# Forms of x summed in PSUM, and the part up to the second pair ordered by the scheduler

## The chip, the core and the metric

The kernel runs on one core of one Trainium2 chip. The metric is device time in microseconds, from the runs of a whole execution. PE is the matrix engine (TensorE), DVE the vector engine, ACT the scalar engine, POOL GpSimd, and SP the engine that issues most transfers. PSUM is the memory into which PE writes; SBUF is the working memory.

## What is computed

An attention without a score matrix feeds a layer of eight experts, and that feeds a feed-forward layer. Batch 4, 8 heads, sequence 576, head width 64; 2304 tokens of width 512.

```python
q_s = exp(q - max(q, -1)); q_s /= sum(q_s, -1) + 1e-9
k_s = exp(k - max(k, 2));  k_s /= sum(k_s, 2) + 1e-9      # over the sequence
x   = q_s @ (k_s^T v)                                     # per batch and head
# x: [2304, 512]
P = exp(x @ w_gate - max); 8 times: rows to 1, columns to 1, times N/E
out = sum over e of P[:, e] * (relu(x @ w1[e]) @ w2[e])   # 8 experts, 512 -> 1024 -> 512
h = out @ w_in; g = h * clip(h + 3, 0, 6) / 6             # 512 -> 2048
return g @ w_out                                          # -> 512
```

## The kernel before

Tokens lie in six groups of 384 (GN); a pair of groups is the unit of the expert products: PAIRS is (0, 1), (3, 4), (2, 5). Batches 0 and 1 give groups 0 to 2 (attention object `t0`), batches 2 and 3 give groups 3 to 5 (`t1`). The hidden width is cut into 20 slices of 512 (16 of experts, 4 of the last layer). A step (s, p) multiplies pair p by slice s: `up_burst` (L845) in two halves of seven sums in PSUM banks A, B, C, D, A, B, C, and `down_tile` (L918) into bank tag d for six token tiles. Values are kept as a high and a low half in f16, and each product is three f16 products.

The up product of a pair uses seven products of combined blocks instead of eight. For each pair x is cut into four blocks, b11 and b21 (channel halves of the first group) and b12 and b22 (of the second), and seven forms of them are stored, with high and low half, in `xop[p]`: QB11, QB21, QB22 are blocks, T1 = b12 - b11, T2 = b22 - T1, T4 = T2 - b21, T3 = b22 - b12. cp = 0, 1 counts two channel quarters of a half, so there are 14 forms in a pair. `combine_steps` (L365) makes them: `xmm` (L593 to L605) multiplies k^T v (`bds`) by the turned q (`qT`, L592) on PE, and ACT writes the sum to SBUF times a power of two `sx`; DVE subtracts (L379); ACT writes the high half (L374) and DVE or POOL the low half (L375).

`sx` comes from the largest element of k^T v over all partitions (`kvmax`, `across_max`, `pow2` at L190 to L199). The third pair has one group of each attention object: group 2's x is kept unscaled in `stage2` and scaled later (L676), with the larger maximum of both.

The order. The code is cut into blocks. Inside `with tc.manual_schedule()` every engine's instructions keep the order of the code; outside, a scheduler orders them at build time, with the order of the code as priority, and waits are set for either. Steps of other work are put in the queue `ticks`, and `tick()` after each product of the burst takes `rate` of them, which interleaves the code. Before the change two hand-ordered blocks stand at the beginning: one up to the first pair's x, and one (from L1110) with w1 and w2 of slice 1, group 2's x, steps (0, 0) and (1, 0), the second attention (`beside`, `pair_steps(1)`) and the down tiles of step (1, 0). Then the steps (0, 1), (0, 2), (1, 1), (1, 2) with the third pair, the gate's logits and the balancing (`sinkhorn_steps`) are scheduled. SP issues the second k (L418), then w1 of slice 1 (L260), the second v (L439), the second q (L418), w2 of slice 1 (L296). The buffers of k and v (`kt`, `vt`) lie in the room of the second and third pair's forms, those of q in `acc`.

Of the kernel before, what the change touches and what calls it, by code (L numbers as in the profile page):

```python
# [40 lines left out]
def tile_attention_moe_ffn(  # L41
# [12 lines left out]
    nc = tc.nc  # L54
    B, H, S, D = q.shape
    NT, DM = out.shape
# [42 lines left out]
    def psm(shape, name, dt=F32):  # L99
        return ps_m.tile(shape, dt, tag="m", name=name)  # L100
# [3 lines left out]

    ident = cpool.tile([P, P], F32, name="ident")
    ones = cpool.tile([P, P], F32, name="ones")
    three = cpool.tile([P, 1], F32, name="three")
    X_W = 7 * 2 * 2 * GN // 2
    W1_W = 7 * 2 * 2 * (FS // 2) // 2
# [10 lines left out]
    bds = cpool.tile([P, 2, NKC, P], F32, name="bds")  # L120
    sx = cpool.tile([P, len(PAIRS), 2], F32, name="sx")
    mx = cpool.tile([P, len(PAIRS)], F32, name="mx")
    prob = cpool.tile([P, NJ, E], F32, name="prob")
    lg = cpool.tile([P, NJ, 2 * E], F32, name="lg")
    win32 = dram.tile([DM, NF * FS], F32, name="win32")
# [42 lines left out]
    def run(steps):  # L168
        for f in steps:
            if f is not None:  # L170
                f()
# [190 lines left out]
        put(back, [], "conv")  # L362


    def combine_steps(p, cp, bs, first=False):  # L365
# [12 lines left out]
        def tt(o, a, b):  # L378
            return lambda: V.tensor_sub(o, a, b)  # L379

        if first:
            return [
                sp(QB11, b11, V), tt(t1, b12, b11),
                lambda: (tt(t2, b22, t1)(), sp(QT2, t2, V)()),
                sp(QT1, t1, V),
                lambda: (tt(t1, t2, b21)(), sp(QT4, t1, V)()),
                sp(QB21, b21, V),
                lambda: (tt(b12, b22, b12)(), sp(QT3, b12, V)()),
                sp(QB22, b22, V),
            ]  # L390
# [17 lines left out]
    def attention(pr):  # L408
# [126 lines left out]
        def kvkeep():  # L535
            nc.vector.tensor_copy(mx[:, pr : pr + 1], st["mm"])
            pow2(st["mm"], sx[:, pr, :], TOP1)
            if pr == 1:
                nc.vector.tensor_max(mx[:, 2:3], mx[:, 0:1], mx[:, 1:2])
                pow2(mx[:, 2:3], sx[:, 2, :], TOP1)  # L540


        gl = lambda g: g % (QR // GJ)
# [36 lines left out]
        def qtr(c, g, src=None):  # L580
            src = t["qn"] if src is None else src
            ps = psm([P, GJ, P], f"qT{c}_{g}")
            for r in range(GJ):
                nc.tensor.transpose(ps[:, r, :], src[:, r * P : (r + 1) * P], ident)
            t["m"] = t.get("m", 0) + 1
            if "rooms" in t:
                qT = t["rooms"][2 + t["m"] % 2]
# [6 lines left out]
        def xmm(c, g, dst, scale):  # L594
            if "rooms" not in t:
                t["x"] = t.get("x", -1) + 1
                ps = ps_u.tile([P, 512], F32, tag="CDAB"[t["x"] % 4], name=f"x{c}_{g}")[:, :GN]
                ps = ps.rearrange("p (r n) -> p r n", n=P)
            else:
                ps = psm([P, GJ, P], f"x{c}_{g}")  # L600
            q3 = t["qT", c, g].rearrange("p (r n) -> p r n", n=P)
            for i in range(2):
                n = slice(i * QP, (i + 1) * QP)
                nc.tensor.matmul(ps[:, :, n], bds[:, i, c, :], q3[:, :, n], start=True, stop=True)  # L604
            nc.scalar.activation(dst, ps.rearrange("p r n -> p (r n)"), AF.Copy, scale=scale)  # L605

        def items(lst):

# [3 lines left out]
            for u in range(n + late):  # L612
                def f(u=u):
# [10 lines left out]
        t["max"] = [lambda: (kvmax(), a()), gap, b, kvkeep]  # L624
        t.update(vcopy=vcopy, v_ones=v_ones, load_k=load_k, load_v=load_v, load_q=load_q, kmax=kmax, ktr=ktr, mT=mT,
                 kback=kback, ksub=ksub, kexp=kexp, kv_=kv, kvout=kvout, qmax=qmax, qsub=qsub, qexp=qexp, qsum=qsum,
                 qn_=qn, qtr=qtr, xmm=xmm, items=items)
        return t

    def call(t):  # L630
# [27 lines left out]
    def unit_items(p, cp, bs):  # L658
        ga, gb = PAIRS[p]
        x = sx[:, p, 0:1]  # L660
        return [(cp, ga, bs[0], x), (cp + 2, ga, bs[1], x), (cp, gb, bs[2], x), (cp + 2, gb, bs[3], x)]

    def pair_steps(p, items):
        steps = []
        for cp in range(2):
            if p < 2:
                bs = (U, R)[cp][:6]
                steps += items(unit_items(p, cp, bs))
            else:
                bs = [stage2[:, cp], stage2[:, cp + 2]] + U[2:6]  # L670
                gb = PAIRS[p][1]

                x = sx[:, 2, 0:1]

                def scaled(b):
                    return lambda: nc.scalar.activation(b, b, AF.Copy, scale=x)  # L676
                if cp == 0:
                    steps += group_steps(t1, gb)
                steps += [scaled(bs[0]), scaled(bs[1])]
                steps += items([(cp, gb, bs[2], x), (cp + 2, gb, bs[3], x)])  # L680
            steps += combine_steps(p, cp, bs)
        return steps

# [290 lines left out]
    with tc.manual_schedule():  # L974
        make_identity(nc, ident)
        nc.vector.memset(ones, 1.0)
        nc.vector.memset(three, 3.0 * KAPPA)
        nc.gpsimd.memset(bds, 0.0)

        t0, t1 = attention(0), attention(1)  # L980
        K = call(t0)
        w2_room = half(acc[:, :NFC, :])
        room1 = half(acc[:, NFC : 2 * GJ + GJ, :])
        U1 = [room1[:, i * GN : (i + 1) * GN] for i in range(6)]
# [34 lines left out]
        def turned(g):  # L1019
            for c in range(NKC + 1):  # L1020
# [15 lines left out]
        run(t0["max"][1:])  # L1036
        t1["load_k"](2)

        bs0, bs1 = U[:6], U1
        it = {(c, g): (c, g, dst, x) for c, g, dst, x in unit_items(0, 0, bs0) + unit_items(0, 1, bs1)}  # L1040
        c0 = combine_steps(0, 0, bs0, first=True)
        c1 = combine_steps(0, 1, bs1, first=True)
        X = lambda c, g: (lambda: t0["xmm"](*it[c, g]))
# [63 lines left out]


    FROM, TO, AGAIN = 6, len(order) - 3 * NF - 3, len(order) - 3 * NF + 2
    with tc.manual_schedule():  # L1110
        w1_1 = w1_steps(1)
        w1_1[0]()
        for i in range(2):
            t1["load_v"](i=i)
        t0["rooms"] = [U[3], U[4], U1[0], U1[1]]
        third = PAIRS[2][0]
        it = t0["items"]([(c, third, stage2[:, c], 1.0) for c in range(NKC)])
        put(ticks, a2, ("w2", 0))
        put(ticks, group_steps(t0, third))
        both = w1_1[4:]  # L1120
        while it or both:
            if both:
                put(ticks, [both.pop(0)])
            if it:
                put(ticks, [it.pop(0)])
        put(ticks, [], ("w1", 1))
        rate[0] = 3
        prev = step(0, 0, None)
        need(("w1", 1))
        t1["load_q"]()  # L1130
        w2_1 = w2_steps(1)
        w2_1[0]()
        t1["rooms"] = R[6:]
        one = beside(t1)
        put(ticks, one[:10])
        put(ticks, w2_1[4:], ("w2", 1))
        put(ticks, one[10:])
        put(ticks, pair_steps(1, t1["items"]), ("x", 1))
        rate[0] = 2
        prev = step(1, 0, prev)  # L1140
        for grp in range(2):
            run(downs(prev, grp))
        need(("x", 1))
        rate[0] = 1
        first_pair, prev = prev, None
# [3 lines left out]
    put(ticks, pair_steps(2, t1["items"]), ("x", 2))  # L1149
    put(ticks, logit_steps(1))  # L1150
    put(ticks, logit_steps(2))
    put(ticks, sinkhorn_steps(), "P")
# [45 lines left out]
```

## Time and profile before

| what | us |
|---|---|
| three runs | 1936.97, 1944.75, 1945.9 |
| median | 1944.75 |
| profiled execution, whole | 1942.0 |
| its span, first to last instruction | 1940.2 |
| PE busy in the span | 1847.7 (95%) |
| DVE busy | 1316.9 (68%) |
| ACT busy | 779.7 (40%) |
| POOL busy | 623.7 (32%) |

The profile is of one execution. Its page has the busy share of each engine in 40 slices of 48.5 us, and tables of groups of instructions. The trace is asked for more: stages (busy time of each engine between two moments), the timeline, waits, and groups by line. Times in it count from the span's start.

### The profile page before, as it was taken

The numbers are of one execution on the slowest core, as the hardware profiler recorded it, in microseconds if no ns is written. First come the engines' busy times: TensorE is split into PE (matmuls) and PEld (weight loads), VectorE is DVE, ScalarE is ACT, GpSimd is POOL, SyncE is SP. The second block draws the span as 40 slices with busy tenths as digits, with TensorE's granted clock in tenths as the row PEclk, the third lists the DMA queues.
The fourth block names the chain that finished last, engine by engine and source line by source line (L and its number), as shares of the span: only waits on it lengthen the run. The fifth ranks groups of instructions, "written<-read, shape, count | busy, mean of one in ns | idle before, by whom it ended". The sixth has DMA issues, their size and how long they took to land.

```text
span 1940.2 us, 26715 instructions
## 1 busy us (share of the span) xinstructions
PE 1847.7 (95%) x10506; PEld 987.0 (51%) x10506; DVE 1316.9 (68%) x2331; ACT 779.7 (40%) x1448; POOL 623.7 (32%) x588
## 2 busy tenths in 40 slices
PE   4569999999999999999999999999999999999999
PEld 3335545555555555555555555555555555555554
DVE  7685665776767667676667676666756897668554
ACT  3534543333434333333434343333333456544342
POOL 3214323433323323333323334242332323323111
PEclk9779999999999999999999999999999999999999
DMA  8710000121020111111111111111100100000001
GB/s 240 119 45 1 1 22 23 43 67 55 23 71 31 63 32 45 55 60 55 39 55 39 55 39 55 39 46 47 60 28 1 44 22 22 23 22 23 1 27 72
DMA packets 48622, 87.71 MB, mean 45 GB/s; under 512 B 12400, under 2 KB 12400, under 8 KB 48496
## 3 DMA queue, kind: packets, MB, share of 16 engines
q1 hardware_dynamic: 46800, 82.47, 14.0%
q10 hardware_dynamic: 1696, 3.54, 0.6%
q8 instruction: 82, 1.34, 0.3%
q14 instruction: 44, 0.36, 0.1%
HBM read 72.89 MB, written 13.11 MB: 44 GB/s over the span
## 4 chain that ended last, share of the span: by engine, by line
PE 79%; DVE 12%; DMA 3%; ACT 2%; issue 2%; POOL 1%; ACTq 0%; SPq 0%; DVEq 0%; POOLq 0%
PE y L918 41%; PE B L845 11%; PE C L845 10%; PE A L845 10%; PE D L845 5%; DVE r L853 2%; DVE w1buf L205 2%; DVE g L868 1%; DMA raw<-in_moe_w_dram 1%; DVE xbuf L375 1%; DVE scr L379 1%; DVE w2buf L205 1%; DVE acc L928 1%; PE x L604 1%; DMA acc<-in_moe_w_dram 1%
## 5 line engine op out<-in xcount | busy, mean ns | idle before, releaser
L918 PE MATMUL y<-w2buf,h 128*128 128x512 f16 x4320 | 980.1, 380 | 0.1
L845 PEld LDWEIGHTS <-w1buf 128*128 128x128 f16 x5040 | 494.9, 98 | 389.7 <-issue 47.6
L918 PEld LDWEIGHTS <-h 128*128 128x128 f16 x4320 | 423.2, 98 | 476.3 <-issue 4.8
L875 POOL TENSOR_TENSOR h<-r,h 128x384 f16<-128x384 f32 x288 | 276.1, 959 | 870.9 <-ACT h L874 799.8
L853 DVE SCALAR_TENSOR_TENSOR r<-B,r 128x384 f32<-128x384 f32 x240 | 133.2, 555 | 252.2 <-PE B L845 243.9
L928 DVE SCALAR_TENSOR_TENSOR acc<-y,cf,acc 128x512 f32<-128x512 f32 x252 | 188.3, 748 | 156.6 <-PE y L918 156.4
L845 PE MATMUL C<-xbuf,w1buf 128*128 128x384 f16 x1440 | 277.5, 329 | 15.2 <-DVE r L853 13.8
L845 PE MATMUL B<-xbuf,w1buf 128*128 128x384 f16 x1440 | 278.8, 330 | 8.0 <-DVE r L853 2.3
L845 PE MATMUL A<-xbuf,w1buf 128*128 128x384 f16 x1440 | 277.2, 328 | 5.4 <-ACT scr L605 4.3
L891 ACT ACTIVATE r<-A 128x384 f32<-128x384 f32 x120 | 58.8, 490 | 337.3 <-PE A L845 337.3
L873 ACT ACTIVATE r<-r 128x384 f32<-128x384 f32 x192 | 100.0, 521 | 165.5 <-DVE r L853 159.1
L874 ACT CAST h<-r 128x384 f16<-128x384 f32 x288 | 147.1, 511 | 8.6
L870 POOL TENSOR_TENSOR h<-g,h 128x384 f16<-128x384 f32 x72 | 67.7, 940 | 255.1 <-ACT h L869 204.5
L845 PE MATMUL D<-xbuf,w1buf 128*128 128x384 f16 x720 | 137.9, 326 | 3.4 <-DVE xbuf L375 1.1
L853 DVE SCALAR_TENSOR_TENSOR r<-C,r 128x384 f32<-128x384 f32 x240 | 132.6, 552 | 11.6 <-PE C L845 1.7
L884 ACT ACTIVATE r<-A 128x384 f32<-128x384 f32 x120 | 58.6, 488 | 203.4 <-PE A L845 203.4
L869 ACT CAST h<-g 128x384 f16<-128x384 f32 x96 | 49.1, 511 | 96.8 <-DVE g L868 96.8
L877 ACT ACTIVATE h<-r 128x384 f16<-128x384 f32 x96 | 50.1, 522 | 92.4 <-DVE r L853 92.4
L878 DVE SCALAR_TENSOR_TENSOR h<-r,h 128x384 f16<-128x384 f32 x96 | 81.5, 849 | 5.5 <-ACT h L877 5.5
L868 DVE SCALAR_TENSOR_TENSOR g<-g,r 128x384 f32<-128x384 f32 x96 | 62.4, 652 | 12.9 <-ACT g L867 10.4
L867 ACT ACTIVATE g<-r,three,zi 128x384 f32<-128x384 f32 x96 | 67.5, 704 | 7.6 <-DVE r L853 3.2
L853 DVE SCALAR_TENSOR_TENSOR r<-D,r 128x384 f32<-128x384 f32 x120 | 66.8, 556 | 3.9
(610 smaller groups left out, 1483.5 us busy)
## 6 DMA issues: line engine op xcount, KB each, us to landing
raw<-in_moe_w_dram SPq DMA_DIRECT2D x31, 1024.0 KB, 5.6
scr<-in_moe_w_in_dram SPq DMA_DIRECT2D x16, 512.0 KB, 4.2
scr<-in_moe_w_out_dram SPq DMA_DIRECT2D x16, 512.0 KB, 3.8
out_dram<-acc SPq DMA_DIRECT2D x18, 256.0 KB, 2.0
win<-scr SPq DMA_DIRECT2D x16, 256.0 KB, 3.4
wout<-scr SPq DMA_DIRECT2D x16, 256.0 KB, 2.2
raw<-win SPq DMA_DIRECT2D x4, 1024.0 KB, 5.0
raw<-wout SPq DMA_DIRECT2D x4, 1024.0 KB, 5.7
```

The source lines that it names most:

```text
L845: nc.tensor.matmul(bank[b], w[:, i, wi, c, fs], x[:, i, xi, c, :], start=(first and n == 0), stop=(last and n == 5), skip_group_check=True,)
L853: nc.vector.scalar_tensor_tensor(out=o, in0=bank[b], scalar=sign * H_DOWN, in1=i1, op0=ALU.mult, op1=ALU.add)
L867: nc.scalar.activation(r, c, AF.Relu, scale=zi, bias=three)
L868: nc.vector.scalar_tensor_tensor(out=r, in0=r, scalar=6.0 * KAPPA, in1=c, op0=ALU.min, op1=ALU.mult)
L870: eng.tensor_sub(h[:, 1, :], r, h[:, 0, :])
L873: nc.scalar.activation(c, c, AF.Relu)
L874: nc.scalar.copy(h[:, 0, :], c)
L875: eng.tensor_sub(h[:, 1, :], c, h[:, 0, :])
L878: nc.vector.scalar_tensor_tensor(out=h[:, 1, :], in0=c, scalar=0.0, in1=h[:, 0, :], op0=ALU.max, op1=ALU.subtract)
L891: nc.scalar.activation(r4, bank["A"], AF.Copy if ffn else AF.Relu, scale=H_DOWN)
L918: nc.tensor.matmul(ps, hs[grp][fc][:, hi, ts_], w[:, wi, fc, :], start=(n == 0), stop=(n == 11))
L928: nc.vector.scalar_tensor_tensor(out=acc[:, j, :], in0=ps, scalar=cf, in1=acc[:, j, :], op0=ALU.mult, op1=ALU.add)
```

## The change

The forms are no longer made in SBUF. k^T v is scaled once, when its scale is known. PE writes a block into a PSUM bank, and adds stored halves of other forms to it with an identity matrix (`plus`) or its negative (`minus`) in f16; ACT writes the high half from PSUM and DVE the low half. The bank of b22 is kept for T2, T4 and T3, which are further sums onto it. In the first pair the two kept banks are A and B and the others C, D and d; in the second they are the two buffers of tag m. The first pair's forms come in another order, as do w1's splits between them. The second pair's eight turned q get eight rooms instead of two, and their turning is written ahead of most forms. The second block is no longer hand-ordered; its text is the same but for that. The third pair's forms are made as before, with factors relative to the scales already in.

```diff
+        nc.scalar.copy(plus, ident)
+        nc.scalar.activation(minus, ident, AF.Copy, scale=-1.0)
         t0, t1 = attention(0), attention(1)
...
         def kvkeep():
             nc.vector.tensor_copy(mx[:, pr : pr + 1], st["mm"])
             pow2(st["mm"], sx[:, pr, :], TOP1)
+            nc.scalar.activation(bds[:, 0], bds[:, 0], AF.Copy, scale=sx[:, pr, 0:1])
+            nc.vector.tensor_scalar_mul(bds[:, 1], bds[:, 1], sx[:, pr, 0:1])
...
+        def xset(ps, c, g):
+            p3 = ps.rearrange("p (r n) -> p r n", n=P)
             q3 = t["qT", c, g].rearrange("p (r n) -> p r n", n=P)
             for i in range(2):
                 n = slice(i * QP, (i + 1) * QP)
+                nc.tensor.matmul(
+                    p3[:, :, n], bds[:, i, c, :], q3[:, :, n], start=(i == 0), stop=(i == 1), skip_group_check=True
+                )
...
+        def forms(p, cp, bank):
...
+            def out_(ps_, qd):
+                nc.scalar.copy(dst[:, qd, 0, cp], ps_)
+                nc.vector.tensor_tensor(out=dst[:, qd, 1, cp], in0=ps_, in1=dst[:, qd, 0, cp], op=ALU.subtract)
+
+            def onto(ps_, qds):
+                for m, qd in qds:
+                    for hl in range(2):
+                        nc.tensor.matmul(
+                            ps_, m, dst[:, qd, hl, cp], start=False, stop=True, skip_group_check=True
+                        )
...
+            return [
+                plain(cp, ga, QB11), f_t1, plain(cp + 2, gb, QB22), f_on(QT2, [(minus, QT1)]),
+                plain(cp + 2, ga, QB21), f_on(QT4, [(minus, QB21)]), f_on(QT3, [(plus, QB21), (minus, QB11)]),
+            ]
...
+    def second_pair(t):
...
+        f = [t["forms"](1, cp, lambda n: psm([P, GN], n)) for cp in range(2)]
...
-        run([X(0, ga), X(1, ga), c0[0], c1[0], a1[0], X(0, gb), X(1, gb), c0[1], c1[1], X(2, gb), X(3, gb), a1[1],
-             c0[2], c1[2], X(2, ga), X(3, ga), a1[2], c0[3], c1[3], a1[3], c0[4], c1[4], a1[4], c0[5], c1[5], a1[5],
-             c0[6], c1[6], a1[6], c0[7], c1[7]])
+        f0 = t0["forms"](0, 0, lasting("A"))
+        f1 = t0["forms"](0, 1, lasting("B"))
+        run([f0[0], f1[0], a1[0], f0[1], f1[1], f0[2], f1[2], a1[1], f0[3], f1[3], a1[2], f0[4], f1[4], a1[3],
+             f0[5], f1[5], a1[4], f0[6], f1[6], a1[5], a1[6]])
...
-    with tc.manual_schedule():
-        w1_1 = w1_steps(1)
-        w1_1[0]()
...
-        t1["rooms"] = R[6:]
...
-        put(ticks, pair_steps(1, t1["items"]), ("x", 1))
...
+    w1_1 = w1_steps(1)
+    w1_1[0]()
...
+    t1["rooms"] = R[8:] + R[:8]
...
+    put(ticks, second_pair(t1), ("x", 1))
```

## Rows read from the trace of the kernel before

**Rows 1.** The page's slices of 48.5 us: busy tenths, granted clock in tenths

```profile
PE   4569999999999999999999999999999999999999
PEclk9779999999999999999999999999999999999999
```

**Rows 2.** Stages: from:to, length, busy (instructions) of PE, PEld, DVE, ACT, POOL; clock; transfers

```profile
42.50:51.50 9.00, 4.34 (x26) 3.82 (x25) 5.51 (x12) 6.49 (x14) 0.00 (x0) 0.95 0.03 9
51.50:135.00 83.50, 48.01 (x206) 25.17 (x206) 65.15 (x109) 39.50 (x70) 18.91 (x18) 0.72 0.47 84
135.00:190.00 55.00, 50.22 (x516) 29.82 (x515) 31.41 (x58) 25.99 (x50) 20.31 (x21) 0.94 0.05 17
190.00:270.00 80.00, 73.99 (x575) 43.95 (x573) 59.67 (x158) 40.43 (x80) 26.04 (x27) 1.00 0.02 4
...
51.50:66.00 14.50, 10.56 (x38) 4.65 (x37) 12.88 (x28) 11.16 (x22) 1.45 (x1) 0.74 0.00 0
```

**Rows 3.** Waits of PE, 51.5 to 135 us: total us, times, longest

```profile
PE kT L463 <- DVE scr L456: 19.2, 4, 9.4
PE C L845 <- DVE r L853: 9.2, 2, 6.1
```

**Rows 4.** Timeline (start, length): scale of x, first burst, step (0, 1)

```profile
42.45 0.14 DVE L199 TENSOR_SCALAR sx<-eb 128x1 int32<-128x1 int32 x1
...
51.55 2.08 PE L845 MATMUL A<-xbuf,w1buf 128*128 128x384 f16 x6 [4.34 <-ACT scr L605]
...
189.52 0.65 PE L845 MATMUL A<-xbuf,w1buf 128*128 128x384 f16 x3
```

**Rows 5.** Timeline: work of later code inside the hand-ordered part

```profile
140.56 1.21 DVE L234 TENSOR_REDUCE am_a__2300<-raw 128x1 f32<-128x1024 f32 x1
...
141.76 1.21 DVE L234 TENSOR_REDUCE am_a__2300<-raw 128x1 f32<-128x1024 f32 x1
...
153.44 1.63 ACT L676 ACTIVATE acc<-acc,sx 128x384 f32<-128x384 f32 x3 [3.59 <-DVE sx L196]
```

**Rows 6.** Timeline: last product of the first v; the second v and q

```profile
30.96 2.66 PE L510 MATMUL kv<-xbuf 64*64 64x65 f32 x88 [3.31 <-issue]
...
66.92 15.21 SPq L439 DMA_DIRECT2D xbuf<-in_v_dram  x16
...
82.24 2.93 SPq L418 DMA_DIRECT2D acc<-in_q_dram  x4
```

**Rows 7.** DVE groups by line, 41 to 190 us: busy us, mean ns, idle before

```profile
L375 DVE TENSOR_TENSOR xbuf<-scr,xbuf 128x384 f16<-128x384 f32 x11 | 7.5, 677 | 3.4 <-ACT xbuf L374 3.3
L379 DVE TENSOR_TENSOR scr<-scr 128x384 f32<-128x384 f32 x8 | 4.5, 559 | 4.4 <-ACT scr L605 4.4
L853 DVE SCALAR_TENSOR_TENSOR r<-B,r 128x384 f32<-128x384 f32 x8 | 4.4, 546 | 1.2 <-PE B L845 1.0 <-ACT r L884 0.2
L375 DVE TENSOR_TENSOR xbuf<-acc,xbuf 128x384 f16<-128x384 f32 x7 | 3.9, 553 | 0.6 <-ACT xbuf L374 0.6
L205 DVE SCALAR_TENSOR_TENSOR w1buf<-raw,ws_a__436,w1buf 128x512 f16<-128x512 f32 x5 | 3.7, 747 | 0.0
```

**Rows 8.** ACT groups by line, 41 to 190 us

```profile
L374 ACT CAST xbuf<-scr 128x384 f16<-128x384 f32 x14 | 6.7, 507 | 4.8 <-DVE scr L379 4.8
L605 ACT ACTIVATE scr<-x,sx 128x384 f32<-128x384 f32 x8 | 4.6, 581 | 4.0 <-DVE sx L199 3.1 <-PE x L604 0.8
L592 ACT COPY xbuf<-qT 128x384 f32<-128x384 f32 x8 | 3.8, 471 | 3.2 <-PE qT L584 3.2
```

**Rows 9.** POOL groups by line, 150 to 196 us: the second pair's low halves

```profile
L375 POOL TENSOR_TENSOR xbuf<-scr,xbuf 128x384 f16<-128x384 f32 x3 | 3.4, 1121 | 2.2 <-ACT xbuf L374 2.2
L375 POOL TENSOR_TENSOR xbuf<-xbuf 128x384 f16<-128x384 f32 x3 | 2.9, 995 | 9.9 <-ACT xbuf L374 9.9
```

**Rows 10.** Chain that ended last (start, length), steady stage: six products of 128x384

```profile
279.86 0.97 PE A L845 x6
```

**Rows 11.** ACT's first issue and table load; stages of the start

```profile
0.74 2.98 ACTq L418 DMA_DIRECT2D xbuf<-in_k_dram  x4
...
20.05 1.28 ACT L496 ACT_TABLE_LOAD   x1 [20.05 <-DMA acc<-in_v_dram]
...
0.00:5.00 5.00, 0.00 (x0) 0.00 (x0) 0.17 (x2) 0.00 (x0) 1.76 (x8) 1.00 0.55 135
5.00:10.00 5.00, 0.45 (x1) 0.18 (x1) 3.08 (x7) 0.00 (x0) 0.00 (x0) 1.00 1.04 242
```

**Rows 12.** Waits of PE, 190 to 270 us

```profile
PE csp L762 <- DVE cs L757: 2.2, 2, 1.5
PE B L845 <- POOL xbuf L375: 2.1, 2, 1.2
```

More of the change, by code (lines that the diff above doesn't have):

```diff
@@ L106, in tile_attention_moe_ffn @@
     ones = cpool.tile([P, P], F32, name="ones")
+    plus = cpool.tile([P, P], F16, name="plus")
+    minus = cpool.tile([P, P], F16, name="minus")
     three = cpool.tile([P, 1], F32, name="three")
@@ L362, in all_conv, with combine_steps @@
         put(back, [], "conv")
-    def combine_steps(p, cp, bs, first=False):
+    def combine_steps(p, cp, bs):
         b11, b21, b12, b22, t1, t2 = bs
@@ L379, in tt @@
             return lambda: V.tensor_sub(o, a, b)
[L381 to L390, printed above, removed]
         return [
@@ L540, in kvkeep @@
                 pow2(mx[:, 2:3], sx[:, 2, :], TOP1)
+                for i in range(2):
+                    nc.vector.tensor_mul(rescale[:, i : i + 1], sx[:, 2, 0:1], sx[:, i, 1:2])
         gl = lambda g: g % (QR // GJ)
@@ L586, in qtr @@
             if "rooms" in t:
[L587 removed]
+                qT = t["rooms"][2 + t["m"] % (len(t["rooms"]) - 2)]
             else:
@@ L626, in attention @@
                  kback=kback, ksub=ksub, kexp=kexp, kv_=kv, kvout=kvout, qmax=qmax, qsub=qsub, qexp=qexp, qsum=qsum,
-                 qn_=qn, qtr=qtr, xmm=xmm, items=items)
+                 qn_=qn, qtr=qtr, forms=forms, items=items)
         return t
@@ L656, in tile_attention_moe_ffn, with norm, one, third_pair @@
     R = [view(xbuf, 2 * X_W + i * GN, [P, GN]) for i in range(10)]
[L658 to L663, printed above, removed]
-        steps = []
-        for cp in range(2):
[L666 to L680, printed above, removed]
+    def second_pair(t):
+        order_ = [(c, g) for cp in range(2) for c, g in ((cp, PAIRS[1][0]), (cp, PAIRS[1][1]),
+                                                         (cp + 2, PAIRS[1][1]), (cp + 2, PAIRS[1][0]))]
+        f = [t["forms"](1, cp, lambda n: psm([P, GN], n)) for cp in range(2)]
+        steps = []
+        held = {}
+        def norm(c, g):
+            t["qn_"](c, g)
+            held[c, g] = t["qn"]
+        for n in range(len(order_) + 1):
+            def one(n=n):
+                if n < len(order_):
+                    norm(*order_[n])
+                if n > 0:
+                    t["qtr"](*order_[n - 1], held[order_[n - 1]])
+            steps.append(one)
+            if n >= 5 and f[0]:
+                steps.append(f[0].pop(0))
+        while f[0] or f[1]:
+            for cp in range(2):
+                if f[cp]:
+                    steps.append(f[cp].pop(0))
+        return steps
+    def third_pair(t):
+        p = 2
+        gb = PAIRS[p][1]
+        steps = group_steps(t, gb)
+        for cp in range(2):
+            bs = [stage2[:, cp], stage2[:, cp + 2]] + U[2:6]
+            def scaled(b):
+                return lambda: nc.scalar.activation(b, b, AF.Copy, scale=rescale[:, 0:1])
+            steps += [scaled(bs[0]), scaled(bs[1])]
+            x = rescale[:, 1:2]
+            steps += t["items"]([(cp, gb, bs[2], x), (cp + 2, gb, bs[3], x)])
             steps += combine_steps(p, cp, bs)
@@ L983, in tile_attention_moe_ffn @@
         room1 = half(acc[:, NFC : 2 * GJ + GJ, :])
-        U1 = [room1[:, i * GN : (i + 1) * GN] for i in range(6)]
+        U1 = [room1[:, i * GN : (i + 1) * GN] for i in range(2)]
         v_room = view(half(acc[:, : NJ // 2, :]), 0, [P, H, QR, D])
@@ L1109, in tile_attention_moe_ffn @@
     FROM, TO, AGAIN = 6, len(order) - 3 * NF - 3, len(order) - 3 * NF + 2
-    with tc.manual_schedule():
-        w1_1 = w1_steps(1)
-        w1_1[0]()
[L1113 to L1132, printed above, removed]
-        t1["rooms"] = R[6:]
[L1134 to L1137, printed above, removed]
-        put(ticks, pair_steps(1, t1["items"]), ("x", 1))
[L1139 to L1145, printed above, removed]
+    w1_1 = w1_steps(1)
+    w1_1[0]()
+    for i in range(2):
+        t1["load_v"](i=i)
+    t0["rooms"] = [U[3], U[4], U1[0], U1[1]]
+    third = PAIRS[2][0]
+    it = t0["items"]([(c, third, stage2[:, c], 1.0) for c in range(NKC)])
+    put(ticks, a2, ("w2", 0))
+    put(ticks, group_steps(t0, third))
+    both = w1_1[4:]
+    while it or both:
+        if both:
+            put(ticks, [both.pop(0)])
+        if it:
+            put(ticks, [it.pop(0)])
+    put(ticks, [], ("w1", 1))
+    rate[0] = 3
+    prev = step(0, 0, None)
+    need(("w1", 1))
+    t1["load_q"]()
+    w2_1 = w2_steps(1)
+    w2_1[0]()
+    t1["rooms"] = R[8:] + R[:8]
+    one = beside(t1)
+    put(ticks, one[:10])
+    put(ticks, w2_1[4:], ("w2", 1))
+    put(ticks, one[10:])
+    put(ticks, second_pair(t1), ("x", 1))
+    rate[0] = 2
+    prev = step(1, 0, prev)
+    for grp in range(2):
+        run(downs(prev, grp))
+    need(("x", 1))
+    rate[0] = 1
+    first_pair, prev = prev, None
     put(ticks, gate_weights())
```

53 lines of the change are left out of this document (38 added, 15 removed).

## The prediction

> **What bounds the kernel now.** I read the page's forty slices first: TensorE is at nine tenths or more from the sixth slice on, so only the first 240 us can give anything back to a change of this kind [rows 1]. The table by stage says where in them [rows 2]. From 190 us on PE is busy at the full granted clock. From 51.5 to 135 us it is busy 48.0 of 83.5 us at a mean clock of 0.72, from 135 to 190 us 50.2 of 55 us at 0.94. Counted at full clock, the PE work of the stage 51.5 to 190 is 48.0 x 0.72 + 50.2 x 0.94 = 81.8 us in 138.5 us: 57 us of the stage are idle time or slow clock, nearly all of it before 135 us. The list of waits names who is late there: DVE, with a transpose of k-maxima behind DVE's 19.2 us in four waits, and the up bursts behind DVE's evictions [rows 3]. DVE is not full either: from 42.5 to 190 us it is busy 5.5 + 65.2 + 31.4 = 102.1 of 147.5 us, a share of 0.69 [rows 2]; it runs in an order written by hand and waits for ACT, PE and loads in turn.
>
> The stage begins when the scale of the first x is known (42.5 us) and ends when the first product of step (0, 1), which needs nothing of the second pair any more, starts at 189.5 us [rows 4]. I call that moment the handoff. Behind it PE has enough ready work, so I price the change as the shift of the handoff, one to one in the span.
>
> **Why the order can move.** The trace of before shows what the scheduler does with work that it may place. w1's absolute maxima for slice 2 and the rescaling of the third pair's raw x both stand in the code behind the hand-ordered part; they run at 140.6 and 153.4 us, inside it [rows 5]. So it pulls later work over the written order into gaps. The change gives it the whole part between the first x and the second pair. What it gets to move is large: the loads of the second v are issued only at 66.9 us, behind the load of a weight slice that has to wait for its buffer, and take 15.2 us of SP issue; q follows at 82.2 us [rows 6]. The room of v is free once the first k^T v is done, at 33.6 us [rows 6]. Queues that this passes: SP, where v may go ahead of w1; DVE, where the maxima over k and over the third group of q can fill waits; ACT and POOL, where exponentials, weight splits and products with 1/sum follow them.
>
> **Forms, per pair.** Removed: 8 ACT evictions of x with scale (0.58 us) and 8 DVE subtractions (0.559 us) [rows 7, 8]. Kept: 14 ACT writes of the high half, now from PSUM; the PSUM copy of the same size costs 0.471 against 0.507 from SBUF, so I count no change [rows 8]. Kept: 14 low halves, now all on DVE with one input in PSUM; the DVE eviction that reads PSUM in the same shape takes 0.546 against 0.553 for the split in SBUF, so again no change in size [rows 7]. In the second pair 6 of them come over from POOL, at about 0.555 on DVE, and leave POOL 6 x 1.06 us lighter [rows 9]. Added on PE: 20 products of 128x384, at 0.97/6 = 0.16 us each, 3.3 us [rows 10]. Added to scale bds, per pair, one ACT and one DVE operation of 128x512: the trace has no such single-input operation, a two-input one of that shape takes 0.75, so 0 to 0.75 and I take the upper end, in the ACT case 0.7 us in front of the first product [rows 7]. The few one-column operations for the rescaling (0.15 us each, two of them) are nothing.
>
> The added products are queued in PE's order behind their own operands: T1 waits for the two halves of QB11, and so on over five links. In the first pair they have PE to themselves, because banks A and B are held until the last form, so the first product of the first burst, at 51.55 us now [rows 4], waits for all forms. DVE needs 14 x 0.555 + 7 x 0.75 = 13.0 us for them and w1's splits; at the share of 0.89 that it has in the stage from 51.5 to 66 us [rows 2] that is 14.6 us. The burst then starts at about 59 us. It loses its head start of six products, and doesn't stop at the seventh as it does now.
>
> **The start.** Two copies for plus and minus stand on ACT ahead of its first DMA issue, now at 0.74 us; they need the identity matrix, and with them the table load moves there from 20.05 us [rows 11]. Its 1.28 us, the identity and two copies of at most 0.47 hold the ACT half of the k loads back by 0 to 2.8 us. The transfer engines are at 0.55 in the first 5 us and full afterwards [rows 11], so the SP half fills some of that, and the exponentials at 20 us no longer stand behind the table load; I take 1.0 us. The start of the stage is 42.5 + 1.0 + 0.7 = 44.2 us.
>
> **The sum.** DVE work up to the handoff: 102.1 - 16 x 0.559 + 6 x 0.555 + 2 x 0.75 = 98.0 us, less the 2.4 us of the slice 2 maxima that needn't come before it: 95.6 us. What share the scheduler reaches is the one number that the trace doesn't hold. In the scheduled stage from 190 to 270 us DVE is at 59.7/80 = 0.75, but with PE as the bound; by hand the densest stretch has 0.89 [rows 2]. I take 0.85, nearer to the denser row, because this stage has independent work for every engine. Then 95.6/0.85 = 112.5 us, and the handoff comes at 156.7 instead of 189.5 us: 32.8 us. PE agrees: 81.8 + 3.3 = 85 us of work from 59 us on ends at 144 us at full clock and at 156 us at a mean clock of 0.88. The next thing that is late is then PE itself, and behind the handoff the third pair and the balancing of the gate, where PE already loses a few us to DVE [rows 12]; those come earlier by the same amount, so no gain and no loss there. The profiled execution took 1942.0 us beside its span of 1940.2, 2.8 us below the median of the three runs. 1942.0 - 32.8 = 1909 us.
>
> The Trainium skill, page "SBUF — State Buffer", section "Who interferes with whom", says that a DVE instruction with two SBUF inputs contends with GpSimd instructions that read SBUF, and one with a single SBUF input doesn't. By that the splits from PSUM would all run at the undisturbed 0.55 instead of the mean of 0.677 that eleven of them show [rows 7], another 1.4 us off the sum; I leave it out.
>
> **The rivals.** (a) *Only the forms pay.* The scheduler doesn't raise DVE's share, as the chain from k to the second x is one of latencies. At 0.69 the 95.6 us end at 182.8 us, 6.7 us earlier: 1935 us. For it: the way from k to the second x is maxima, transposes, exponentials, products, a scale and the forms, one after the other; against it: the pulled work above and PE's share in the scheduled stage. (b) *Slower: PE's order blocks.* In the second pair the forms share two PSUM buffers with the turned q, and one is held over each chain. If the 14 forms and 8 turned q each stall the matmuls behind them for the ACT copy and the DVE split, that is 14 x (0.47 + 0.55) + 8 x 0.47 = 18 us [rows 7, 8]; if the clock then falls to the 0.72 of the stage before [rows 2], the 47.2 us of full-clock work of the stage 135 to 190 take 65.6 instead of 50.2, 15 us more. On top of (a) 1935 + 33 = 1968 us. It decides once such stalls add up to more than what filling gives, 33 us; below that the kernel is still faster. Against it: in the stage that is scheduled already, no PE wait is longer than 1.5 us [rows 12]. (c) *The scheduler follows its priority*, which is the old order, and what the forms save goes into the later first burst and the ACT queue: 1942 us.
>
> The Trainium skill, page "TensorE: Matmul & The Clock Gate", section "Step-by-step: what each phase is for", says that matmuls stay in program order and only weight loads are pulled ahead. That is the rule behind rival (b): by it a form's matmul that waits holds every burst product placed after it, and the time would be 1968 us if nothing were placed in between. The trace agrees on the order: one wait of an up product for an eviction of DVE lasts 6.1 us, and PE runs nothing in it [rows 3].
>
> **How the numbers follow.** The forecast has 0.70; its own range runs from 1895 us (handoff at 144 us, where PE at full clock ends) to 1925 us (DVE at 0.75, handoff at 172 us). Rival (a) has 0.15, with times from 1925 to 1940; (b) 0.11; (c) 0.04. The range from 1894 to 1942 leaves out (b) and the thin ends. A measurement of this kernel can tell about 0.5%, 9.7 us, from no change. Faster by more: 0.70 and half of (a), 0.77. Within: the rest of (a) and (c), 0.12. Slower: 0.11.
>
> **What would show it.** Right: the loads of the second v issued before 60 us; DVE's share from 44 us to the handoff at 0.8 or more; the first product of step (0, 1) near 157 us; the first burst starting near 59 us; PE's mean clock up to the handoff above 0.8. Forms wrong: DVE splits from PSUM longer than 0.6 us, or PE waits for the high and low halves of a form beyond 1.5 us each. Start wrong: the scale of the first x known later than 45 us. The forecast falls if the handoff lies beyond 173 us, or if it comes early and PE then idles before 270 us for the third pair or the gate, more than the 6 us of now.

## The result and the profile after

The kernel after takes 1916.9 us (median of four runs, 1916.7 to 1919.3), the kernel before 1942.6 in the four runs beside it: a ratio of 0.9876, with a 95% interval from 0.9861 to 0.9890. It is faster by 1.2%, less than forecast: 1916.9 against 1909, inside the range. The profiled execution took 1916.67 us, its span is 1914.9.

The page's slices of 48.5 us, as in [rows 1] (busy tenths, granted clock in tenths):

```profile
PE   3799999999999999999999999999999999999999
PEclk9899999999999999999999999999999999999999
```

Only the first three slices changed: PE reaches nine tenths in the third slice, where [rows 1] have it in the fourth (not the sixth, as the prediction's first paragraph says), and it is emptier in the first. The stages, with the columns of [rows 2] (the first and the last answer to rows there, the middle two are the stage of the forecast by its new ends):

```profile
51.50:135.00 83.50, 70.88 (x640) 45.64 (x641) 77.94 (x145) 51.68 (x92) 29.69 (x28) 0.93 0.47 92
57.60:164.30 106.70, 97.87 (x782) 60.28 (x781) 89.29 (x163) 65.33 (x121) 35.53 (x34) 0.98 0.29 63
74.30:164.30 90.00, 84.45 (x717) 50.37 (x716) 74.08 (x129) 52.04 (x96) 33.43 (x32) 1.00 0.29 69
190.00:270.00 80.00, 75.42 (x501) 40.63 (x498) 50.77 (x138) 35.04 (x65) 22.67 (x26) 1.00 0.05 14
```

In the 83.5 us from 51.5 to 135, PE is busy 70.9 us at a mean clock of 0.93, against 48.0 at 0.72 [rows 2]; DVE 77.9 instead of 65.2. The three moments of [rows 4], from the timeline (start, length): the scale of the first x, the first products into bank C and into A, and step (0, 1):

```profile
57.60 0.14 DVE L202 TENSOR_SCALAR sx<-eb 128x1 int32<-128x1 int32 x1
...
68.94 0.50 PE L901 MATMUL C<-xbuf,w1buf 128*128 128x384 f16 x2
...
74.34 1.14 PE L901 MATMUL A<-xbuf,w1buf 128*128 128x384 f16 x6
...
164.28 1.14 PE L901 MATMUL A<-xbuf,w1buf 128*128 128x384 f16 x6
```

The handoff moved from 189.52 to 164.28 us, by 25.2; the span shrank by 25.3. So all of the gain lies ahead of the handoff. But the scale of the first x, which starts the stage, comes 15.2 us later than in [rows 4]: the stage itself is 106.7 instead of 147.1 us long, 40.4 us shorter, and 15.2 of these were lost before it began.

PE's waits answer to [rows 3] (us in total, times, longest), first from 57.6 to 164.3 us, then from 164 to 245 us, the stretch that answers to [rows 12]:

```profile
PE C L901 <- DVE r L909: 3.8, 2, 3.2
PE f L619 <- DVE xbuf L614: 1.9, 2, 1.1
...
PE csp L818 <- DVE cs L813: 2.2, 2, 1.5
PE B L901 <- POOL xbuf L378: 2.1, 2, 1.2
```

The 19.2 us behind DVE's maxima of k are gone. Behind the handoff nothing changed: the same two waits with the same sizes as in [rows 12]. SP's issues show how far the loads went ahead, as in [rows 6]:

```profile
34.58 2.07 SPq L432 DMA_DIRECT2D xbuf<-in_v_dram  x2
36.74 3.75 SPq L411 DMA_DIRECT2D xbuf<-in_k_dram  x4
40.54 18.20 SPq L432 DMA_DIRECT2D xbuf<-in_v_dram  x10
...
79.94 11.26 SPq L411 DMA_DIRECT2D acc<-in_q_dram  x4
```

The second v is issued from 34.6 us on; it stood at 66.9 [rows 6]. The second q hardly moved (79.9 against 82.2 us). Last, the groups of the forms (busy us, mean ns, idle before), which answer to [rows 7, 8, 10]:

```profile
L614 DVE TENSOR_TENSOR xbuf<-f,xbuf 128x384 f16<-128x384 f32 x24 | 12.6, 551 | 7.4 <-ACT xbuf L613 7.4
L613 ACT CAST xbuf<-f 128x384 f16<-128x384 f32 x24 | 11.0, 480 | 10.3 <-PE f L597 5.3 <-PE f L619 4.8
L531 ACT ACTIVATE bds<-bds,sx 128x512 f32<-128x512 f32 x2 | 1.4, 722 | 0.0
L532 DVE TENSOR_SCALAR bds<-bds,sx 128x512 f32<-128x512 f32 x2 | 1.2, 609 | 0.0
```

### The profile page after: what moved, and what is told of

Same layout as the page of the kernel before. It is cut to its first block, busy times and chain, and to the rows that moved or that the text cites. A ratio compares the mean times of both kernels' runs of the same rounds, so it can differ in the third digit from the quotient of the medians.

```text
span 1914.9 us, 26755 instructions
## 1 busy us (share of the span) xinstructions
PE 1844.5 (96%) x10546; PEld 988.3 (52%) x10546; DVE 1309.2 (68%) x2325; ACT 773.7 (40%) x1436; POOL 616.9 (32%) x582
## 3 DMA queue, kind: packets, MB, share of 16 engines
q8 instruction: 82, 1.34, 0.3%
## 4 chain that ended last, share of the span: by engine, by line
PE 79%; DVE 14%; DMA 2%; ACT 2%; issue 1%; POOL 1%; SPq 0%; ACTq 0%; DVEq 0%
PE y L974 41%; PE B L901 11%; PE C L901 10%; PE A L901 10%; PE D L901 5%; DVE r L909 2%; DVE w1buf L208 2%; DMA acc<-in_q_dram 1%; DVE g L924 1%; DMA raw<-in_moe_w_dram 1%; DVE w2buf L208 1%; DVE scr L382 1%; DVE acc L984 1%; DVE xbuf L378 1%; DVE acc L553 1%
## 5 line engine op out<-in xcount | busy, mean ns | idle before, releaser
L901 PE MATMUL B<-xbuf,w1buf 128*128 128x384 f16 x1440 | 274.5, 326 | 5.7 <-DVE r L909 2.4
L933 ACT ACTIVATE h<-r 128x384 f16<-128x384 f32 x96 | 50.1, 522 | 92.3 <-DVE r L909 92.3
```

Of the source, the lines that this page charges most:

```text
L901: nc.tensor.matmul(bank[b], w[:, i, wi, c, fs], x[:, i, xi, c, :], start=(first and n == 0), stop=(last and n == 5), skip_group_check=True,)
```

## The experiments

The gain has two candidates, the order and the forms; the loss at the start has two as well, the copies on ACT and work that the scheduler pulls ahead of the scale. In all runs but e3 the span is 1750 to 1752 us longer than the moment of the handoff (before 1940.2 - 189.5 = 1750.7, after 1914.9 - 164.3 = 1750.6; in e3 the first products of step (0, 1) run among the last forms, so the moment marks no boundary there). So each run is read by three numbers: the scale of the first x, the length of the stage from it to the handoff, and the time.

| kernel | scale known | stage | PE, DVE busy in it | time, us | ratio to before |
|---|---|---|---|---|---|
| before | 42.45 | 147.1 | 102.6, 102.1 (from [rows 2], to 190) | 1942.6 | |
| after | 57.60 | 106.7 | 97.9, 89.3 | 1916.9 | 0.988 |
| e3: after, second block by hand | 50.1 | (span 1946.9) | | 1949.1 | 1.004 |
| e4: before, second block scheduled | 47.3 | 107.6 | 92.2, 98.0 | 1907.4 | 0.982 |
| e1: after, late copies | 49.35 | 106.1 | 98.3, 89.0 | 1908.4 | 0.983 |
| e2: before, early copies | 49.65 | 145.0 | 99.8, 101.8 | 1949.9 | 1.004 |
| e5: after, held | 49.8 | 111.8 | 99.1, 99.4 | 1914.6 | 0.986 |
| e6: late copies, held | 42.7 | 112.5 | 100.4, 98.3 | 1907.4 | 0.982 |
| e9: e4, held | 42.5 | 112.5 | 92.8, 105.9 | 1908.8 | 0.983 |
| e7: e1, more on DVE | 49.6 | 114.5 | 101.5, 101.4 | 1917.0 | 0.987 |
| e8: e1, more on PE | 50.3 | 113.1 | 104.8, 89.1 | 1917.4 | 0.987 |
| e10: e1, w2 halves on POOL | 49.6 | 111.9 | 99.9, 88.3 | 1914.9 | 0.986 |

**Which part is the gain: e3 and e4.** The forms without the order (the second block of the kernel after put back under the hand-written order):

```diff
-    w1_1 = w1_steps(1)
+    with tc.manual_schedule():
+        w1_1 = w1_steps(1)
...
```

> The changed kernel with the second block in the written order again: forms in PSUM without the scheduler. Theory 1 (the gain of 25 us is the scheduler's; forms save DVE 8.9 us in a stage in which it is not full, and the loads on ACT start behind two copies): the scale of the first x is known near 50 us instead of 42.5, the first product of step (0, 1) starts between 182 and 195 us, PE's busy share from 51.5 to 135 us stays below 0.7, time 1935 to 1948 us. Rival (the forms are the gain, as they take two links of DVE out of each block's way to xop): first product of step (0, 1) before 175 us, time below 1928 us.

It took 1949.1 us, ratio 1.0040 [1.0025, 1.0055]: slower than before by 0.4%, just past the 1935 to 1948 of theory 1. PE's waits from 50 to 199 us are those of [rows 3] again:

```profile
PE kT L456 <- DVE scr L449: 18.8, 4, 8.5
PE C L901 <- DVE r L909: 9.2, 2, 6.1
```

And the order without the forms, the mirror image:

```diff
-    with tc.manual_schedule():
-        w1_1 = w1_steps(1)
+    w1_1 = w1_steps(1)
...
```

> The kernel before with its second block left to the scheduler and nothing else: forms still made in SBUF, no copies ahead of the loads. Theory 1: DVE has 9 us more to do and the start is early (scale of the first x between 45 and 50 us, as the third group's work is pulled ahead of it); first product of step (0, 1) between 160 and 172 us, time 1913 to 1924 us. Rival (the forms are the gain): time above 1935 us.

It took 1907.4 us, ratio 0.9824 [0.9809, 0.9839], better than theory 1 said and better than the kernel after. The whole gain is the order; the rival that the forms carry it is refuted from both sides. Which part of the order carries it, the earlier loads of the second v or the filled waits, was not tried apart. Its stage (columns of [rows 2]):

```profile
47.30:154.90 107.60, 92.23 (x743) 56.56 (x742) 97.95 (x173) 71.33 (x134) 45.12 (x40) 0.97 0.29 67
```

DVE is at 98.0/107.6 = 0.91 there, PE at 0.86. In the kernel after it is the other way round: DVE 0.84, PE 0.92. Both stages are as long, within 1 us.

**Why the start is late: e1 and e2.** The two copies go behind ACT's loads, with nothing else changed:

```diff
         nc.gpsimd.memset(bds, 0.0)
-        nc.scalar.copy(plus, ident)
-        nc.scalar.activation(minus, ident, AF.Copy, scale=-1.0)
...
         t0["load_v"](v_room)
+        nc.scalar.copy(plus, ident)
+        nc.scalar.activation(minus, ident, AF.Copy, scale=-1.0)
```

> The changed kernel with the two copies that make plus and minus moved behind ACT's issue of the loads; the order of DVE up to the first x is the same. Theory 1 (the copies and the table load hold ACT's loads back, the SP half runs ahead alone, and q lands 7.6 us later; behind it PE is the bound, at 84.5 of 90 us): the first maximum over q starts near 20.4 us instead of 28.0, the scale of the first x is known near 50 instead of 57.6 us, the first product of step (0, 1) starts near 157 instead of 164.3 us, time 1908 to 1911 us. Rival 2 (DVE's total work is the bound, so an early start only moves idle time): scale near 50 us, but the first product of step (0, 1) after 162 us, time 1914 to 1917. Rival 3 (the loads are late because more of them were pulled ahead on SP): nothing moves, 1917 us.

1908.4 us, ratio 0.9831 [0.9816, 0.9845], as theory 1 said: the scale comes at 49.35 instead of 57.60, the handoff at 155.5 instead of 164.3. ACT's queue in the timeline of the kernel after (start, length of the issue):

```profile
0.73 1.28 ACT L1035 ACT_TABLE_LOAD   x1 [0.73 <-PEq L1251]
1.34 0.72 ACTq L411 DMA_DIRECT2D xbuf<-in_k_dram  x1
2.03 0.30 ACT L1035 CAST plus<-ident 128x128 f16<-128x128 f32 x1
2.10 0.63 ACTq L411 DMA_DIRECT2D xbuf<-in_k_dram  x1
2.23 0.30 ACT L1036 ACTIVATE minus<-ident 128x128 f16<-128x128 f32 x1
4.72 5.77 ACTq L411 DMA_DIRECT2D xbuf<-in_k_dram  x2
14.26 1.27 ACTq L411 DMA_DIRECT2D acc<-in_q_dram  x2
```

And in e1:

```profile
0.74 2.68 ACTq L411 DMA_DIRECT2D xbuf<-in_k_dram  x4
5.12 2.88 ACTq L411 DMA_DIRECT2D acc<-in_q_dram  x2
10.18 8.52 ACTq L411 DMA_DIRECT2D acc<-in_v_dram  x4
```

The first two issues slip by 0.6 us each, the third by 2.6 (4.72 against 2.14) and the fourth by 7.1 (9.88 against 2.79), and ACT's half of q goes out at 14.3 instead of 5.1 us. The first maximum of q on DVE, which waits for it, starts at 27.99 instead of 20.01 us. The other direction, the kernel before with the two copies in front, otherwise unused:

```diff
         nc.gpsimd.memset(bds, 0.0)
+        nc.scalar.copy(plus, ident)
+        nc.scalar.activation(minus, ident, AF.Copy, scale=-1.0)
```

> The kernel before with the two copies for plus and minus put ahead of ACT's first load issue, and nothing else of the change (plus and minus are then read by nobody). My theory: the table load and the copies hold ACT's half of the k and q loads back, by the 7.6 us at which the kernel after got its first maximum of q later (20.39 to 27.99 us). Then the scale of the first x comes at 49 to 50.5 us instead of 42.45, the first product of step (0, 1) at 196 to 198 instead of 189.5, and the time is 1948 to 1950 us. Rival 1: only with the scheduled order do the copies cost something, because by hand DVE has other work to do first: the scale stays at 42.5 to 44 us and the time at 1941 to 1944. Rival 2: the start is later but the hand-ordered stage has waits that swallow it: scale at 49 to 50, time 1942 to 1945.

1949.9 us, ratio 1.0038 [1.0023, 1.0053]. The scale comes at 49.65 (+7.2), the first product of step (0, 1) at 194.60 (+5.1): the theory holds, the hand-written order swallows 2 us of it. Beside e3 this says one thing more: e3 has the same copies, and 1949.1 against 1949.9 us is no difference that these runs can tell (each ratio is known to 0.0015, 3 us, either way), so no gain or cost of the forms by themselves shows.

**The other half of the late start: e5 and e6.** In e1 the scale is still at 49.35 instead of 42.45, with loads and copies as before. The DVE timeline shows what stands there: the scheduler has put the third group's maximum, subtraction and sum and the first maxima of the second k ahead of the scale. Three memsets of a few columns, placed behind the scale in the code and writing what this work writes first, keep it back:

```diff
             pow2(st["mm"], sx[:, pr, :], TOP1)
+            if first:
+                nc.vector.memset(t["qm"][:, :, 6:9], 0.0)
+                for i in range(2):
+                    nc.vector.memset(scr[:, i * DM : i * DM + 2], 0.0)
```

> The changed kernel with three small memsets on DVE behind the scale of the first x, into places that the third group's maxima and the second k's maxima write, so that these can't be pulled ahead of the scale. Theory 1 (pulled work costs the start 4.8 + 2.7 us, and PE is the bound behind it): the scale is known near 50 us instead of 57.6, the first product of step (0, 1) between 158 and 163 us instead of 164.3, since some 8 us of DVE work come back into a stage in which DVE has a share of 0.84; time 1910 to 1916 us. Rival 2 (DVE's work is the bound): the first product of step (0, 1) at 164 us or later, time 1917 to 1922 us.

1914.6 us, 0.9864 [0.9848, 0.9881], inside theory 1's range: the scale is 7.8 us earlier than in the kernel after, the handoff only 2.6, because 10.1 us of DVE work came back into the stage (99.4 against 89.3) and made it 5.1 us longer. With both causes taken away, the edit of e1 and this one together:

> The kernel after with the copies behind ACT's loads and with the three small memsets that keep the third group's and the second k's maxima from being pulled ahead of the scale: both causes of the late start taken away at once. The scale of the first x should be known at 42 to 43.5 us. Theory 1 (the start is all that was mis-sized): the stage keeps the 106.1 us that it has with late copies, the handoff comes at 149 us and the time is 1900 to 1903 us. Theory 2 (PE and DVE are both nearly full in the stage, so work that is kept from the start comes back behind it): the stage is 111 to 113 us, the handoff at 153 to 155.5 us, the time 1905 to 1909, no better than late copies alone (1908.4).

1907.4 us, 0.9821 [0.9806, 0.9835]: theory 2. The stage of e5, from the scale to the handoff:

```profile
49.80:161.60 111.80, 99.12 (x784) 60.85 (x785) 99.36 (x177) 66.88 (x122) 37.86 (x36) 0.98 0.36 72
```

And that of e6:

```profile
42.60:155.10 112.50, 100.39 (x784) 61.94 (x785) 98.34 (x177) 66.89 (x122) 37.71 (x36) 0.97 0.36 73
```

Between e1 and e6 the scale moves by 6.7 us and the handoff by 0.3. So with the loads in time the pulled work is a shift of work and costs next to nothing (behind the late loads, holding it back brought the 2.6 us of e5), while the copies, which add idle time, cost all they take in the scheduled order. The same holds without the forms, with the memsets in e4:

> The kernel before (forms in SBUF, no copies) with its second block left to the scheduler, and the three small memsets that keep the third group's and the second k's maxima from being pulled ahead of the scale. The scale should be known at 42.5 to 43.5 us instead of 47.3. Theory (PE and DVE fill the stage together, so an earlier start by pulled work alone gives nothing): handoff 153 to 156 us, 1905.5 to 1909 us, the same as without the memsets (1907.4). Rival (the start counts here, DVE has room): handoff 150 to 151, 1902 to 1904 us.

1908.8 us, 0.9831 [0.9816, 0.9846], against 1907.4 without the memsets: the theory. Its stage:

```profile
42.50:155.05 112.55, 92.75 (x741) 56.90 (x740) 105.93 (x181) 72.67 (x135) 44.44 (x40) 0.94 0.32 71
```

**What fills the stage: e7 and e8.** To price a microsecond of each engine in e1's stage, e7 writes 15 low halves of weights twice on DVE:

```diff
         nc.scalar.activation(hi, src, AF.Copy, scale=scale)
-        nc.vector.scalar_tensor_tensor(out=lo, in0=src, scalar=scale, in1=hi, op0=ALU.mult, op1=ALU.subtract)
+        for _ in range(reps):
+            nc.vector.scalar_tensor_tensor(out=lo, in0=src, scalar=scale, in1=hi, op0=ALU.mult, op1=ALU.subtract)
```

> The kernel after with late copies, and the low halves of w1 and w2 of slice 1 and of w2 of slice 0 written twice by DVE: 15 splits more, by the groups of the late-copies run 4.7 + 2.3 + 3.0 + 2.7 = 12.7 us of DVE work, all in the stage and nobody's operand changed. Theory: with the forms in PSUM, PE is what fills the stage (84.5 of 89.4 us busy from 66 us on; DVE 89.0 of 106.1, 17 us free), so the time rises by 0 to 4 us: 1908 to 1913, handoff 155.5 to 160. Rival: DVE sets the end, and 12.7 us come out as 10 to 13: 1918 to 1922, handoff 166 to 168.

and e8 repeats the second pair's turns and block products on PE:

```diff
-            for r in range(GJ):
+            for r in tuple(range(GJ)) * (2 if pr == 1 and g in PAIRS[1] else 1):
                 nc.tensor.transpose(ps[:, r, :], src[:, r * P : (r + 1) * P], ident)
...
-            for i in range(2):
+            for i in (0, 1) * (2 if pr == 1 and g in PAIRS[1] else 1):
```

> The kernel after with late copies, and the second pair's eight turns of q (0.49 us each) and eight block products (0.84 us each) done twice by PE with the same result: 8 x 0.49 + 8 x 0.84 = 10.6 us of PE work more in the stage. Theory: PE fills the stage, so the time rises by 8 to 11 us: 1916 to 1920, handoff 164 to 167. Rival: DVE's chain of maxima, splits and evictions sets the end and PE has room for it: 1908 to 1912, handoff 155 to 159.

The stage of e1:

```profile
49.35:155.46 106.11, 98.30 (x781) 60.94 (x780) 88.98 (x163) 66.05 (x121) 34.88 (x34) 0.96 0.28 65
```

That of e7:

```profile
49.60:164.20 114.60, 101.50 (x782) 61.69 (x781) 101.42 (x178) 65.89 (x121) 36.83 (x34) 0.94 0.27 60
```

And that of e8:

```profile
50.20:163.30 113.10, 104.77 (x837) 68.46 (x836) 89.10 (x163) 66.20 (x121) 34.87 (x34) 0.98 0.26 60
```

e7: 1917.0 us, and the theory that DVE has 17 us free falls, but the rival's 1918 to 1922 is not reached either. 101.4 - 89.0 = 12.4 us more on DVE made the stage 114.5 - 106.1 = 8.4 us longer, 0.68 for each. A part of this is the clock: in e7 PE runs at the lower of its two levels (0.50, 1.2 GHz) from 134 to 140 us, after two microseconds without a product; in e1 it does so from 120 to 122 us, after a like pause.

e8: 1917.4 us, in the range of its theory. The repeated products add 7.5 us to their groups (less than the 10.6 worked out from single lengths, as their records overlap), and PE's busy time grows by 6.5, as its other products run 1.0 us shorter: from 60 us on e8 has the full clock throughout (1.00), which e1 has not. The stage is 7 us longer, 0.9 to 1.1 for each. Neither engine alone is the bound.

Pairs that were not built for it give DVE a like price: e6 against e1 has 9.4 us more DVE work in a stage 6.4 us longer (0.68), e9 against e4 8.0 in 4.9 (0.61), e5 against after 10.1 in 5.1 (0.50). They are no clean confirmation, since in them the start of the stage moves too. All these prices rest on one profiled execution each, and four executions of e1 spread over 3.7 us, so they are rough.

**Taking work off DVE: e10.** POOL is busy 35 of 106 us, so the eight low halves of w2 went there, with ACT scaling the slice in place first:

```diff
+                nc.scalar.activation(rw[:, c], rw[:, c], AF.Copy, scale=st["s"][:, 0:1])
+                nc.scalar.copy(dst[:, 0, c], rw[:, c])
+                nc.gpsimd.tensor_sub(dst[:, 1, c], rw[:, c], dst[:, 0, c])
```

> The kernel after with late copies, and the low halves of the eight w2 splits of slices 0 and 1 made by POOL instead of DVE (ACT scales the slice in place first, 8 operations of 0.7 us more for it). It takes 3.0 + 2.7 = 5.7 us from DVE and gives POOL, busy 34.9 of 106 us, some 8 x 1.1 = 9 us. Theory: 12.7 us of DVE work more cost 8.6 us, 0.68 for each, so 5.7 less give 3.9: 1904 to 1906 us, handoff 151 to 153. Rival 1: the price holds only upwards, as PE (98.3 of 106.1 us) is the floor: 1907.5 to 1909.5. Rival 2: POOL's reads stretch DVE's operations with two SBUF inputs and the later w2 halves hold the down products up: 1910 to 1915.

1914.9 us, 0.9863 [0.9847, 0.9880]: rival 2. Its stage:

```profile
49.60:161.50 111.90, 99.94 (x781) 62.09 (x780) 88.30 (x155) 69.72 (x129) 44.52 (x42) 0.95 0.28 62
```

DVE has exactly the eight operations fewer that were moved (155 against e1's 163), which took 5.7 us, and its busy time fell by only 0.7 (88.98 to 88.30). By the times of their groups, the other 155 together grew by 3.7 us (91.8 to 95.5; groups overlap, so they add up to more than the busy time). The clearest of them is the subtraction of q's maxima, an operation with two SBUF inputs, in e1:

```profile
L553 DVE TENSOR_TENSOR acc<-acc,qm 128x1536 f32<-128x1536 f32 x3 | 5.2, 1729 | 0.0
```

and in e10:

```profile
L560 DVE TENSOR_TENSOR acc<-acc,qm 128x1536 f32<-128x1536 f32 x3 | 6.2, 2063 | 0.0
```

The longest of these three, 2.69 us from 116.32 us on, overlaps two of the new POOL operations (117.36 to 121.15 us). The 24 splits with one input in PSUM did not grow (553 to 552 ns).

PE's longest wait in e10 from 44 to 160 us is behind the maximum of k^T v:

```profile
PE cm_kv L184 <- DVE kvm L531: 7.2, 2, 4.1
```

But 4.1 us of it belong to the first k^T v, ahead of the scale, and stand in e1 as well:

```profile
46.06 0.77 PE L184 MATMUL cm_kv<-ident,kvm 128*128 128x128 f32 x2 [4.09 <-DVE kvm L524]
```

New is the other, of 3.1 us behind the second k^T v; PE's wait for POOL's products with 1/sum also grew, from 0.3 to 2.6 us. From the scale to the handoff PE is idle for 12.0 us in e10 and 7.8 in e1, and busy 1.6 us longer. So POOL being late with its own work is a rival to POOL slowing DVE; they were not tried apart. The other half of rival 2, down products held up, isn't seen: PE waits before none of them in the stage.

## Why the prediction was right, and where it missed

**The bound and the handoff: right.** Idle time and slow clock ahead of the handoff were what could be had, and each microsecond of the handoff was one of the span, in every run but e3, which has no such moment. Behind it PE waited for the same things as before.

**The order: right, and its size near, in part by luck.** The second v is issued at 34.6 us (said: before 60), DVE's share from the scale to the handoff is 89.3/106.7 = 0.84 (taken: 0.85), the mean clock is 0.98 (said: above 0.8), PE's busy time from the first full burst on is 84.5 us at full clock (worked out: 85). e4 shows that this is the order's doing. The kernel nearest to the forecast's premises is e6, where the start isn't late: its scale at 42.7 and its stage of 112.5 us stand beside the forecast's 44.2 and 112.5. That the stage agrees to the tenth is luck: e6 has 98.3 us of DVE work at a share of 0.87, the forecast 95.6 at 0.85. Two terms of its DVE work missed in opposite directions. The forms take 7.6 us off DVE (e9's 105.9 to e6's 98.3) where 4.1 were summed, and the scheduled stage holds 3.8 us more of other work than the hand-ordered one (e9's 105.9 against 102.1) where 2.4 were taken off.

**The start: the step that failed.** The forecast put 1.0 us on the two copies and the table load, with 2.8 as the upper end, and 0.7 on the scaling of bds (0.72 on ACT, right). The copies cost 8.0 us at the first maximum of q (27.99 to 20.01) and 8.8 us at the handoff (e1 against after), 7.2 and 5.1 in the hand-written order (e2). With 8.8 instead of 1.0 the forecast would have been 1917 us; that is the size of the whole miss. By the prediction's own signs the start was wrong beyond 45 us, and it came at 57.6; the first full burst (74.3 instead of 59) and the handoff (164.3 instead of 157) are late with it. What was wrong is the form of the estimate: it summed the lengths of what stands ahead of the issue and took the transfer engines' busy share for a guarantee that nothing is lost. The share is full in both kernels, the bytes are not. The stretch 5 to 14 us in the stage table (the last two columns are the transfers' busy share and GB/s), before:

```profile
5.00:14.00 9.00, 2.29 (x11) 1.14 (x11) 6.19 (x15) 0.00 (x0) 0.00 (x0) 1.00 1.05 297
```

After:

```profile
5.00:14.00 9.00, 1.55 (x6) 0.66 (x6) 3.62 (x10) 0.00 (x0) 0.00 (x0) 1.00 1.06 248
```

And in e1:

```profile
5.00:14.00 9.00, 2.62 (x11) 1.14 (x11) 6.57 (x15) 0.00 (x0) 0.00 (x0) 1.00 1.05 312
```

**Pulled work.** The forecast had not counted that the scheduler would also put 7 us of work ahead of the scale, though [rows 5] show it doing just that. It mattered little: the work is done once, and e6 and e9 give the same times with it kept back. It does mean that the two ends of the miss are unequal: the scale came 13.4 us later than said, the stage was 5.8 us shorter.

**The forms: each row right, their gain wrong.** The splits from PSUM took 0.551 us (taken: 0.555; wrong if above 0.6), the longest wait of PE for a half was 1.1 us (limit 1.5), the first burst into A started 16.7 us after the scale (worked out: 14.8), with C and D pulled ahead of it. But I counted the forms as DVE work saved and hid their added products behind it. They take 9.0 us from DVE (e4's 98.0 to e1's 89.0) and give PE 6.1 (92.2 to 98.3). At the measured prices that is 0.68 x 9.0 = 6.1 us won and 0.9 to 1.1 x 6.1 = 5.5 to 6.7 lost, and indeed e1 and e4 lie within 1 us. The pair with equal starts, e9 and e6, gives 7.6 us less on DVE and 7.6 more on PE in stages of one length, where these prices would make e6's 2 to 3 us longer; they hold no closer than that. A cost on PE is hidden only while PE is the idle one, and the change itself ended that.

**DVE's share as a model.** Dividing DVE's work by a share of 0.85 made each microsecond of it worth 1.18. The runs say 0.5 to 0.7 once PE is at 0.9. The level came out near by the terms above that partly cancel; by these prices, a forecast for more work from the same formula would have been wrong by about half of the difference. The range's lower end was summed wrong: a handoff at 144 us gives 1942.0 - 45.5 = 1896.5 us, not 1895, and nothing hangs on it.

**The rivals.** (a) is out as a mechanism: the forms in the hand-written order give 1949 us, not 1935, and with the copies' share taken off (e2) nothing. (b), that PE's order blocks, isn't seen: PE's waits for halves of forms add up to 2.2 us in the stage. (c) falls with e4.

The Trainium skill, page "SBUF — State Buffer", section "Who interferes with whom", has it that a DVE instruction with one SBUF input doesn't contend with GpSimd, outside its 2-port modes, and one with two does while GpSimd reads SBUF. The runs agree on both: the 24 splits of the largest group from PSUM have a mean of 551 ns, where eleven of those from SBUF had 677 before [rows 7], and in e10 eight more operations of POOL on SBUF came with the growth of the subtraction above from 1729 to 2063 ns, while the splits from PSUM stayed as they were. What would need a run of its own is whether all of the 3.7 us there is this.

## What to carry to other kernels

Before pricing work saved on one engine, ask how full the other will be in the new order: here 1 us of DVE was worth 0.5 to 0.7 us and 1 us of PE about 1, and an exchange of one for the other gave nothing. Work that the scheduler pulled ahead was only moved; the delay of the first loads was idle time and was paid in full in the scheduled order (8.8 us) and for 5.1 of 7.2 us by hand, so even short work is better placed behind the first DMA issues of a queue. The better kernel of this study is the change with the two copies behind the loads (1908.4 us, or 1907.4 with the work held back), no different from the order alone without the forms (1907.4).

## What the runs showed of the hardware

Not expected: where each load is issued half from SP and half from ACT, a late start of ACT's issues came with a lower rate of all transfers. With ACT's first issue 0.6 us later (1.34 instead of 0.74) its third load of k went out at 4.72 us, behind SP's first load of q at 3.70, its fourth at 9.88 instead of 2.79, and its half of q at 14.26 instead of 5.12; from 5 to 14 us the transfers moved 248 GB/s instead of 297 to 312 at a busy share of 1.05 to 1.06. The Trainium skill, page "DMA: Bandwidth & Descriptors", section "Issuing engines are not separate DMA queues", says that issuing from several engines only saves the issuing sequencer's time. By that the slip of 0.6 us at the first issue would be estimated to cost about as much; the runs have 7 to 8 us at the first operation that needs both halves, which is nearer to the slip of the later issues (7.1 us at the fourth). Why ACT's third issue waits from 2.7 to 4.7 us while the engine itself is free, and why a full busy share moves fewer bytes, stays open; the copies and the table load that they bring were only tried together.
